# Where the first values are asked for: ScalarE's queue for two sets of values, and the third pair's q and k ahead of the second pair's values

## The chip, the core and the metric

The kernel runs on one core of a Trainium2 chip. The core has five engines that run their own instruction streams in order and wait for each other by semaphores: TensorE (PE, matrix products; PEld are its weight loads), VectorE (DVE), ScalarE (ACT), GpSimd (POOL) and SyncE (SP), which here only issues transfers. Transfers between HBM and the core's memory (SBUF) run on 16 DMA engines. The metric is the time of one execution on the device in microseconds (us); smaller is better.

## What is computed

Attention over 4 batches, 8 heads, 576 positions and 64 columns per head, a dense two-layer network with a softmax-weighted activation on its 2304 rows, and a mixture of eight experts. The shortened reference:

```
scores = (q @ k.T) / 8                      # per batch and head, 576 x 576
heads 0-3: keep 0 <= i - j < 32             # local heads
heads 4-7: keep i >= j and i % 32 == j % 32 # strided heads
attn = softmax(scores) @ v                  # -> x, 2304 x 512
h = x @ w_in                                # w_in 512 x 1024, float64
solu = h * softmax(h); ln = layernorm(solu) * g_ln
x = ln @ w_out                              # w_out 1024 x 512, float64
e = argmax(x @ w_gate + modality_bias[modality_id])
out = p_e * (relu(x @ w1[e]) @ w2[e])       # 8 experts
```

## The kernel before

Heads are worked on two at a time. A pair (batch, two heads) has a tile of q (`qn`), of k (`kn`) and of v (`vn`); 16 pairs are done in the order of `order` in `attention_slots` (L623). For batch 0 the order is two strided pairs first, then two local pairs. "The first pair" and "the second pair" below are the two strided ones, "the third" is the first local one. For each pair TensorE transposes q and k (into `ptq`; ScalarE copies them to `qT` and `kz`), forms scores (`S`), VectorE, ScalarE and GpSimd make the softmax (`exc` and `pc` for the first two pairs, `ex` and `pT` for the others), and TensorE multiplies by the values (into `po`, `bank`, `poy`); ScalarE and VectorE then split the result into a high and a low part (`xTH`, L496, and `xTL`, L497).

Beside that runs the preparation of w_in. It arrives as eight pieces of 128 x 1024 words (halves of float64 numbers, 512 KB each, tile `raw`). `f64_piece` makes float32 of a piece: a product `mag` on ScalarE (L292) or GpSimd (L294), two or three bit operations on VectorE (L301, L302, L304), then a cast on ScalarE (L312, `winH`) and a difference on VectorE or GpSimd (L314, `winL`). The pieces of w_out are prepared by the same function.

What sets the order: the kernel is written as a list of steps (`STAGES`, `W_IN_AT` and other tables of numbers), and a scheduler of the framework then orders each engine's instructions by a model of their durations. Buffers come from pools: `vn` has two, `qn` and `kn` together three (the second pair's k lies elsewhere), the `raw` tiles three and some borrowed ones. An instruction that needs a buffer waits until its last user is done. Each transfer also takes one of eight completion semaphores in turn (`DMAHW0` to `DMAHW7` in the rows of the order below) and waits, on the engine that issues it, for the transfer that had the same semaphore before, eight transfers earlier.

The start is set by the list `START` (L88): `q0` means `load_pair` of the first pair, which asks for q and k and, for the first two pairs, keeps the request for v back; `v0` issues that request (`get(v, vn)`, four transfers of 72 KB, L367); `r0` asks for the first piece of w_in. Behind it stand the four transpositions of the first pair. All these transfers are issued by SyncE. The third pair's `load_pair` comes later, out of `stage_t`, when the second pair's transposition is written. For a local pair, `load_pair` asks for q, k (L388) and v (L395, L397) together, GpSimd clears a corner of `vn` (L393), and `shift_values` copies parts of it within SBUF (L406).

Of the kernel before, what the change touches and what calls it, by code (L numbers as in the profile page):

```python
# [9 lines left out]
F32 = mybir.dt.float32  # L10
F32R = mybir.dt.float32r
I32 = mybir.dt.int32
U32 = mybir.dt.uint32
AF = mybir.ActivationFunctionType
ALU = mybir.AluOpType
# [13 lines left out]
def tile_attention_moe_moe2(  # L29
# [15 lines left out]
    nc = tc.nc  # L45
    B, H, S, D = q.shape
    NT, DM = out.shape
    NE, _, FF = w1.shape
    P = 128
# [8 lines left out]
    QUAD = 32  # L58
    RES = STRIDE // SG
    NR = SP_ // RES  # L60
# [20 lines left out]
    MAG_ON = 'AAAPAAPAAPPPAAPA'  # L81
    SIGN_ON = 'DDDDDDDDDDDDDDDP'
    W_IN_LOW = 'DDDDDPDP'
    LOW_ON = 'PPDDDPDD'
    KN1_HOME = True
    ANCHOR = False
    EXS = 4
    START = ['q0', 'q1', 'r0', 'r1', 'v0', 'v1']  # L88
    COMPACT_ON = 'P'
    E_BUFS = 2  # L90
    SO_BUFS = 2
# [74 lines left out]
    def warm(n, after=False):  # L166
        wide = ident.bitcast(mybir.dt.bfloat16)
        for _ in range(n):
            mm = nc.tensor.matmul(warm_out, wide[:, 0:P], wide, start=True, stop=True)
            if after and last_mm[0]:  # L170
                queue_after(mm, last_mm[0])
            last_mm[0] = mm
# [9 lines left out]
    def note(x):  # L182
        newest[x.ins.engine] = x

    def behind_newest(x):
        if ANCHOR and x.ins.engine in newest:
            queue_after(x, newest[x.ins.engine])

    def build_masks():
# [93 lines left out]
            nc.sync.dma_start(raw, w_out32[:, f])  # L283
            raw_out[f] = raw

    def f64_piece(raw, tm, tw, by_act, sgn="D"):
        hi, lo = raw[:, :, 1], raw[:, :, 0]
        mag = mp.tile([P, 512], F32, name="mag", tag=tm, bufs=TAG_BUFS.get(tm, 2))
        w = mp.tile([P, 512], F32, name="wf", tag=tw, bufs=TAG_BUFS.get(tw, 2))
        wi = w.bitcast(I32)  # L290
        if by_act:
            behind_newest(nc.scalar.activation(mag, hi.bitcast(F32), AF.Copy, scale=REBIAS))  # L292
        else:
            behind_newest(nc.gpsimd.tensor_tensor(  # L294
                mag, hi.bitcast(F32), rebias.to_broadcast([P, 512]), ALU.mult))
        if sgn == "P":
            nc.gpsimd.tensor_tensor(hi.bitcast(F32), hi.bitcast(F32), zeros.to_broadcast([P, 512]), ALU.mult)
            behind_newest(nc.vector.scalar_tensor_tensor(
                wi, mag.bitcast(I32), 3, hi, ALU.logical_shift_left, ALU.bitwise_or))
        else:  # L300
            behind_newest(nc.vector.tensor_scalar(wi, mag.bitcast(I32), 3, None, ALU.logical_shift_left))  # L301
            nc.vector.scalar_tensor_tensor(  # L302
                wi, hi, -2147483648, wi, ALU.bitwise_and, ALU.bitwise_or)
        nc.vector.scalar_tensor_tensor(  # L304
            wi, lo, 29, wi, ALU.logical_shift_right, ALU.bitwise_or)
        return w

    def prep_w_in(i):
        c, hf = divmod(IN_ORDER[i], 2)
        cs = slice(hf * 512, hf * 512 + 512)  # L310
        w = f64_piece(raw_in.pop(i), IN_MAG_TAG, "so", MAG_ON[i] == "A", SIGN_ON[i])
        nc.scalar.copy(winH[:, c, cs], w)  # L312
        low = nc.gpsimd if W_IN_LOW[i] == "P" else nc.vector
        low.tensor_tensor(winL[:, c, cs], w, winH[:, c, cs].bitcast(F32), ALU.subtract)  # L314
# [37 lines left out]
    def load_pair(b, hp, v_later=None):  # L352
# [8 lines left out]
        if hp >= H // 4:  # L361
            def get(src, dst):
                dst = dst[:, 0:2 * SG * D].rearrange("p (h x) -> p h x", h=2)
                if b == 0 and src is v:
                    parts = src[b, h0:h0 + 2].rearrange("h (a r i) d -> r a h (i d)", r=RES, i=SG)
                    for r in range(RES):
                        loaded[n_] = nc.sync.dma_start(dst[r * QUAD:r * QUAD + NR], parts[r])  # L367
                else:
                    loaded[n_] = nc.sync.dma_start(
                        dst[:SP_], src[b, h0:h0 + 2].rearrange("h (p i) d -> p h (i d)", i=SG))  # L370

            loaded[n_] = None
            get(q, qn)
            get(k, kn)
            if v_later:
                v_later.append(lambda: get(v, vn))
            else:
                get(v, vn)
            return qn, kn, vn[:, 0:2 * SG * D].rearrange("p (h t d) -> p h t d", h=2, d=D)
# [242 lines left out]
    def attention_slots():  # L622
# [6 lines left out]
        nat, tr, live = {}, {}, {}  # L629

        def load(n):
            if n < len(order):
                nat[n] = load_pair(*order[n])

        def transpose(n, part):
            if n < len(order):
                if part == 0:
                    tr[n] = alloc_pair(n, order)
                transpose_part(*order[n], part, *nat[n][0:2], *tr[n])
                if part == 3 and order[n][1] < H // 4:  # L640
                    shift_values(nat[n][2])

        late_v = [[None], [None]]
        for what in START:
            n_ = int(what[1])
            if what[0] == "q":
                nat[n_] = load_pair(*order[n_], late_v[n_])
            elif what[0] == "v":
                late_v[n_][1]()
            else:  # L650
                fetch_w_in(n_)
        for part in range(4):
            transpose(0, part)
            warm(WARM)
        pts = {}

        def stage_a(n):
# [929 lines left out]
```

## Time and profile before

| | us |
|---|---|
| median of 3 runs (lowest to highest) | 641.71 (638.81 to 642.04) |
| the profiled execution | 641.9 |
| its span | 640.2 |
| TensorE busy in the span | 597.3 |
| VectorE, ScalarE, GpSimd busy | 350.9, 278.6, 133.2 |

The span is the stretch of the profile from the first to the last recorded work; the profiled execution's own time is 1.7 us longer. Times in the rows below are counted from the span's start. The granted clock of TensorE (PEclk) is given as a share of its full 2.4 GHz; a DMA share is the mean busy share of the 16 DMA engines, which can be a little above one where packets overlap.

### The profile page before, as it was taken

The numbers are of one execution on the slowest core, as the hardware profiler recorded it, in microseconds if no ns is written. First come the engines' busy times: TensorE is split into PE (matmuls) and PEld (weight loads), VectorE is DVE, ScalarE is ACT, GpSimd is POOL, SyncE is SP. The second block draws the span as 40 slices with busy tenths as digits, with TensorE's granted clock in tenths as the row PEclk, the third lists the DMA queues.
The fourth block names the chain that finished last, engine by engine and source line by source line (L and its number), as shares of the span: only waits on it lengthen the run. The fifth ranks groups of instructions, "written<-read, shape, count | busy, mean of one in ns | idle before, by whom it ended". The sixth has DMA issues, their size and how long they took to land. (4 is left out here: it accounts for less than half of the span.)

```text
span 640.2 us, 14649 instructions
## 1 busy us (share of the span) xinstructions
PE 597.3 (93%) x5675; PEld 532.5 (83%) x5675; DVE 350.9 (55%) x1058; ACT 278.6 (44%) x653; POOL 133.2 (21%) x197
## 2 busy tenths in 40 slices
PE   6468899999999999999999999999999999999992
PEld 5356678998889988889888999989888888899892
DVE  6695696498567975677388744117264553121120
ACT  4345675555554656545165522124335352221220
POOL 2234221021011231024023412310111203012101
PEclk9999889999999999999999999999999999999997
DMA  7846540033322124110045200445456463012010
GB/s 203 249 136 170 152 121 21 20 90 95 105 55 55 38 72 110 38 36 17 18 136 160 84 34 23 117 159 158 148 165 198 132 203 101 21 51 67 22 44 24
DMA packets 48435, 61.65 MB, mean 96 GB/s; under 512 B 29361, under 2 KB 32971, under 8 KB 48333
## 3 DMA queue, kind: packets, MB, share of 16 engines
q1 hardware_dynamic: 41469, 44.09, 24.4%
q0 software_dynamic: 4272, 11.57, 5.7%
q10 hardware_dynamic: 2592, 4.72, 2.0%
q8 instruction: 53, 0.87, 0.6%
q14 instruction: 49, 0.40, 0.2%
HBM read 48.40 MB, written 10.26 MB: 92 GB/s over the span
## 5 line engine op out<-in xcount | busy, mean ns | idle before, releaser
L1146 PE MATMUL py<-w2H,winL 128*128 128x512 f32 x288 | 91.8, 395 | 0.0
L1190 PE MATMUL pf<-xTH,w1H 128*128 128x256 f32 x288 | 82.2, 286 | 1.0 <-DVE yo L1294 1.0
L1190 PE MATMUL pf<-xTL,w1H 128*128 128x256 f32 x288 | 81.7, 284 | 0.6 <-DVE xTL L1125 0.6
L1190 PE MATMUL pf<-xTH,w1L 128*128 128x256 f32 x288 | 81.5, 283 | 0.0
L1197 DVE SCALAR_TENSOR_TENSOR winL<-pf,winL 128x512 fp32r<-128x512 f32 x36 | 24.9, 692 | 95.2 <-ACT winL L1196 95.1
L1146 PEld LDWEIGHTS py<-w2H,winL 128*128 128x128 f32 x288 | 53.5, 188 | 10.6
L715 PE MATMUL ph<-winH,xTH 128*128 128x512 f32 x144 | 60.3, 419 | 1.2 <-DVE so L732 1.2
L1196 ACT ACTIVATE winL<-pf 128x512 fp32r<-128x512 f32 x36 | 21.5, 598 | 87.2 <-PE pf L1190 87.2
L715 PE MATMUL ph<-winL,xTH 128*128 128x512 f32 x144 | 58.3, 405 | 0.0
L1190 PEld LDWEIGHTS pf<-xTH,w1H 128*128 128x128 f32 x288 | 56.3, 196 | 2.2 <-ACT yo L1292 1.4
L1190 PEld LDWEIGHTS pf<-xTL,w1H 128*128 128x128 f32 x288 | 56.3, 196 | 1.3 <-DVE xTL L1125 1.0
L715 PE MATMUL ph<-winH,xTL 128*128 128x512 f32 x144 | 57.2, 402 | 0.0
L1190 PEld LDWEIGHTS pf<-xTH,w1L 128*128 128x128 f32 x288 | 56.3, 196 | 0.0
L1156 POOL DMA_INDIRECT out_dram<-yo,idx x14 | 14.1, 1004 | 141.3 <-ACT yo L1153 123.7
L797 PE MATMUL pa<-woH,nH 128*128 128x264 f32 x144 | 42.2, 293 | 1.0 <-ACT nH L786 1.0
L797 PE MATMUL pa<-woH,nL 128*128 128x264 f32 x144 | 42.6, 296 | 0.1
L797 PE MATMUL pa<-woL,nH 128*128 128x264 f32 x144 | 41.3, 287 | 0.0
L797 PE MATMUL pb<-woH,nH 128*128 128x256 f32 x144 | 41.1, 285 | 0.0
L797 PE MATMUL pb<-woH,nL 128*128 128x256 f32 x144 | 41.0, 285 | 0.0
L797 PE MATMUL pb<-woL,nH 128*128 128x256 f32 x144 | 40.7, 283 | 0.0
L559 POOL TENSOR_TENSOR ex<-ex,rd 72x288 f32<-72x288 f32 (+2 forms) x28 | 18.8, 673 | 76.6 <-DVE rd L550 45.9
L715 PEld LDWEIGHTS ph<-winH,xTH 128*128 128x128 f32 x144 | 27.9, 194 | 6.7 <-DVE so L732 1.7
(297 smaller groups left out, 1529.3 us busy)
## 6 DMA issues: line engine op xcount, KB each, us to landing
raw<-in_moe_w_dram SPq DMA_DIRECT2D x36, 512.0 KB
y_d<-yt ACTq DMA_DIRECT2D x18, 256.0 KB
raw<-in_moe_w_in_dram SPq DMA_DIRECT2D x8, 512.0 KB
raw<-in_moe_w_out_dram SPq DMA_DIRECT2D x8, 512.0 KB
qn<-in_q_dram SPq DMA_DIRECT2D x8, 288.0 KB
kn<-in_k_dram SPq DMA_DIRECT2D x8, 288.0 KB
qn<-in_q_dram SPq DMA_DIRECT2D x16, 144.0 KB
kn<-in_k_dram SPq DMA_DIRECT2D x16, 144.0 KB
```

Of the source, the lines that this page charges most:

```text
L559: note(nc.gpsimd.tensor_tensor(ex, ex, rd.unsqueeze(2).to_broadcast([nq, nt, nk]), ALU.mult))
L715: nc.tensor.matmul(ph, a[:, c, ts_], w[:, c, cs], start=n == 0, stop=n == 3 * KD - 1)
L797: nc.tensor.matmul(p, a[:, f], w[:, f, cols], start=n == 0, stop=n == 3 * KF - 1)
L1146: mm_ = nc.tensor.matmul(p, a[:, f, s], x, start=n == 0, stop=n == 3 * KF - 1)
L1156: nc.gpsimd.indirect_dma_start(out=out[:, :], out_offset=indirect(idx[:, col, 2:3].bitcast(U32)), in_=o, in_offset=None, bounds_check=NT - ...
L1190: mm = nc.tensor.matmul(p[:, u], a[:, c, fs], x[:, c], start=n == 0, stop=n == 3 * KD - 1)
L1196: last[0] = (nc.scalar.activation(hH[:, f2s], p, AF.Relu), nc.vector.scalar_tensor_tensor(hL[:, f2s], p, 0.0, hH[:, f2s].bitcast(F32), ALU ...
L1197: nc.vector.scalar_tensor_tensor(hL[:, f2s], p, 0.0, hH[:, f2s].bitcast(F32), ALU.max, ALU.subtract))
```

## The change

`START` is written anew, the first two pairs' values are issued by ScalarE (`V_QUEUE`), and `load` leaves out a pair that is loaded already. `t0` in the list stands for the four transpositions of the first pair, which stood behind the list. The parameter `ANCHOR` becomes a tuple of pieces; empty, it does nothing, as `False` did.

```
-    ANCHOR = False
+    ANCHOR = ()
+    V_QUEUE = 'scalar'
     EXS = 4
-    START = ['q0', 'q1', 'r0', 'r1', 'v0', 'v1']
+    START = ['q0', 'q1', 'r0', 'v0', 'r1', 't0', 'q2', 'v1']
...
                     for r in range(RES):
-                        loaded[n_] = nc.sync.dma_start(dst[r * QUAD:r * QUAD + NR], parts[r])
+                        loaded[n_] = getattr(nc, V_QUEUE).dma_start(dst[r * QUAD:r * QUAD + NR], parts[r])
...
         def load(n):
-            if n < len(order):
+            if n < len(order) and n not in nat:
                 nat[n] = load_pair(*order[n])
...
-            if what[0] == "q":
-                nat[n_] = load_pair(*order[n_], late_v[n_])
+            if what[0] == "t":
+                for part in range(4):
+                    transpose(0, part)
+                    warm(WARM)
+            elif what[0] == "q":
+                nat[n_] = load_pair(*order[n_], late_v[n_] if n_ < 2 else None)
             elif what[0] == "v":
                 late_v[n_][1]()
             else:
                 fetch_w_in(n_)
-        for part in range(4):
-            transpose(0, part)
-            warm(WARM)
```

`q2` asks for all three tensors of the third pair. Line numbers after the change are one or two higher. The values of the third pair take the second buffer of `vn`, so those of the second pair take the first pair's buffer.

SyncE at the start of the program, before (72 rows are a strided pair's q and k, 96 a local pair's, 18 the first two pairs' values, 128x1024 a piece of w_in):

```order
L369 DMA qn<-in_q_dram 72x2x512
L369 DMA kn<-in_k_dram 72x2x512
L369 DMA qn<-in_q_dram 72x2x512
L369 DMA kn<-in_k_dram 72x2x512
L277 DMA raw<-in_moe_w_in_dram 128x1024 x2
L367 DMA vn<-in_v_dram 18x2x512 x8
L277 DMA raw<-in_moe_w_in_dram 128x1024
L388 DMA qn<-in_q_dram 96x2x192 x2
L388 DMA kn<-in_k_dram 96x2x192 x2
L388 DMA qn<-in_q_dram 96x2x192 x2
```

The same place after the change, with the semaphores that each row waits for (a third transfer of values, of 64 rows, then the third and another piece follow):

```order
L370 DMA kn<-in_k_dram 72x2x512
L370 DMA qn<-in_q_dram 72x2x512
L370 DMA kn<-in_k_dram 72x2x512
L278 DMA raw<-in_moe_w_in_dram 128x1024 [waits DMAHW0_49]
L278 DMA raw<-in_moe_w_in_dram 128x1024 [waits DMAHW1_49]
L389 DMA qn<-in_q_dram 96x2x192 [waits DMAHW2_49,PE_49]
L389 DMA qn<-in_q_dram 96x2x192 [waits DMAHW3_49]
L389 DMA kn<-in_k_dram 96x2x192 [waits DMAHW4_49,PE_49]
L389 DMA kn<-in_k_dram 96x2x192 [waits DMAHW5_49]
L396 DMA vn<-in_v_dram 128x4x64 [waits DMAHW6_49]
L396 DMA vn<-in_v_dram 128x4x64 [waits DMAHW7_49]
```

The eight transfers of values have left SyncE, and the third pair's q, k and values stand ahead of the third piece of w_in; the first two pieces now wait for one landing each, since ScalarE's four transfers have taken four of the eight semaphores.

ScalarE some 38 us into the run, at the end of the first pair's products with values, before:

```order
L292 ACTIVATE mag<-raw 128x512
L312 CAST winH<-wf 128x512
L496 CAST xTH<-po 128x18x4
L496 CAST xTH<-bank 128x18x4
L496 CAST xTH<-poy 128x18x4 x2
L446 COPY kz_112<-ptq 64x288 x2
```

And after:

```order
L497 CAST xTH<-po 128x18x4
L293 ACTIVATE mag<-raw 128x512
L497 CAST xTH<-bank 128x18x4
L497 CAST xTH<-poy 128x18x4
L313 CAST winH<-wf 128x512
L368 DMA vn<-in_v_dram 18x2x512 x4
L497 CAST xTH<-poy 128x18x4
L447 COPY kz_112<-ptq 64x288 x4
```

The second pair's values are issued there; the first pair's are ScalarE's first instructions.

GpSimd some 43 us into the run, up to the softmax of the third pair (`ex`; `mag` are products for pieces of w_out, `tabi` a table that is cleared), before:

```order
L234 MEMSET tabi 128x176x2
L235 MEMSET tabi 128x176
L314 TENSOR_TENSOR winL<-wf,winH 128x512
L474 TENSOR_TENSOR exc<-exc,rd 128x4x18
L533 TENSOR_TENSOR ex<-ex,mx 128x256
L294 TENSOR_TENSOR mag<-raw,rebias 128x512 x2
L559 TENSOR_TENSOR ex<-ex,rd 128x256
```

And after:

```order
L235 MEMSET tabi 128x176x2
L236 MEMSET tabi 128x176
L315 TENSOR_TENSOR winL<-wf,winH 128x512
L475 TENSOR_TENSOR exc<-exc,rd 128x4x18
L295 TENSOR_TENSOR mag<-raw,rebias 128x512 x2
L534 TENSOR_TENSOR ex<-ex,mx 128x256
L560 TENSOR_TENSOR ex<-ex,rd 128x256
```

The two products of w_out have moved from behind the first subtraction to ahead of it.

## Rows read from the trace of the kernel before

**Rows 1.** Page, span in 40 slices: busy tenths of TensorE, its clock

```profile
PE   6468899999999999999999999999999999999992
PEclk9999889999999999999999999999999999999997
```

**Rows 2.** Stretches (us): length, busy us of engines (count), PEclk, DMA share, GB/s

```profile
0.00:66.00 66.00, 41.12 (x909) 33.44 (x911) 44.27 (x143) 29.14 (x83) 21.39 (x59) 1.00 0.68 191
66.00:70.00 4.00, 4.00 (x71) 2.86 (x63) 1.28 (x6) 3.63 (x10) 1.26 (x3) 0.57 0.71 175
...
90.80:97.60 6.80, 6.54 (x49) 5.15 (x48) 5.72 (x20) 5.67 (x16) 1.98 (x3) 0.52 0.16 46
97.60:640.00 542.40, 526.54 (x4470) 474.68 (x4468) 281.56 (x839) 225.34 (x504) 103.46 (x125) 0.99 0.28 83
```

**Rows 3.** Stretches of the start, the same columns (PE, PEld, DVE, ACT, POOL)

```profile
11.20:13.70 2.50, 1.96 (x40) 1.65 (x40) 2.50 (x10) 1.91 (x6) 0.32 (x1) 1.00 0.74 164
...
16.00:20.30 4.30, 0.00 (x0) 0.00 (x0) 0.26 (x2) 0.01 (x1) 0.00 (x0) 1.00 1.08 240
20.30:25.30 5.00, 4.68 (x134) 4.09 (x134) 4.31 (x20) 3.92 (x10) 1.36 (x3) 1.00 1.01 334
```

**Rows 4.** Timeline of SyncE: start, us, line, tile<-source, count

```profile
3.56 8.37 SPq L367 DMA_DIRECT2D vn<-in_v_dram  x8
...
12.82 0.81 SPq L388 DMA_DIRECT2D qn<-in_q_dram  x2
...
21.12 0.34 SPq L277 DMA_DIRECT2D raw<-in_moe_w_in_dram  x1
...
50.00 0.33 SPq L283 DMA_DIRECT2D raw<-in_moe_w_out_dram  x1
...
61.16 2.10 SPq L391 DMA_DIRECT2D qn<-in_q_dram  x2
```

**Rows 5.** Waits of SyncE until 60 us: us in total, times, longest

```profile
SPq L367 <- DMA kn<-in_k_dram: 2.3, 2, 1.2
SPq L367 <- DMA raw<-in_moe_w_in_dram: 2.0, 2, 1.1
```

**Rows 6.** Timeline near 20 us, three engines; in brackets idle time before and its releaser

```profile
20.29 0.66 ACT L292 ACTIVATE mag<-raw 128x512 f32<-128x512 f32 x1 [5.35 <-DMA raw<-in_moe_w_in_dram]
...
20.61 1.57 PE L158 MATMUL ptq<-ident,qn 96*64 96x96 f32 x12 [5.26 <-DMA qn<-in_q_dram]
...
20.99 0.43 DVE L301 TENSOR_SCALAR wf<-mag 128x512 int32<-128x512 int32 x1 [4.73 <-ACT mag L292]
```

**Rows 7.** Timeline near 27 us, GpSimd and VectorE

```profile
26.92 1.04 POOL L294 TENSOR_TENSOR mag<-raw,rebias 128x512 f32<-128x512 f32 x1 [1.53 <-DVE rd L469]
...
28.00 0.96 DVE L301 TENSOR_SCALAR wf<-mag 128x512 int32<-128x512 int32 x2 [1.14 <-POOL mag L294]
```

**Rows 8.** Stretch from 30 to 40 us, columns of rows 2

```profile
30.00:40.00 10.00, 5.17 (x116) 4.42 (x116) 9.55 (x24) 6.44 (x20) 2.47 (x4) 1.00 0.34 108
```

**Rows 9.** Timeline: ScalarE, TensorE and VectorE around the second pair's products with values

```profile
39.23 0.36 ACT L496 CAST xTH<-poy 128x72 fp32r<-128x72 f32 x2
...
42.17 0.39 PE L158 MATMUL po<-pc,vn 18*64 18x18 f32 x2 [4.03 <-DVE xTL L497]
...
49.07 0.19 DVE L497 TENSOR_TENSOR xTL<-po,xTH 128x72 fp32r<-128x72 f32 x1
```

**Rows 10.** Timeline around the third pair's first softmax

```profile
50.55 0.61 POOL L533 TENSOR_TENSOR ex<-ex,mx 128x256 f32<-128x256 f32 x1 [1.74 <-DVE mx L529]
...
52.97 0.18 DVE L550 RECIPROCAL rd<-den 128x4 f32<-128x4 f32 x1
...
53.09 1.04 POOL L294 TENSOR_TENSOR mag<-raw,rebias 128x512 f32<-128x512 f32 x1 [0.18 <-DMA raw<-in_moe_w_out_dram]
...
54.75 0.69 PE L154 MATMUL pP<-ident,ex 128*128 128x128 f32 x2
```

**Rows 11.** Timeline of TensorE at 65 us

```profile
65.38 0.44 PE L154 MATMUL ptq<-ident,qn 96*128 96x96 f32 x3 [2.55 <-DMA qn<-in_q_dram]
```

More of the change, by code (lines that the diff above doesn't have):

```diff
@@ L183, in note, with behind_newest @@
         newest[x.ins.engine] = x
-    def behind_newest(x):
-        if ANCHOR and x.ins.engine in newest:
+    def behind_newest(x, piece):
+        if piece in ANCHOR and x.ins.engine in newest:
             queue_after(x, newest[x.ins.engine])
@@ L284, in fetch_w_out, with f64_piece @@
             raw_out[f] = raw
-    def f64_piece(raw, tm, tw, by_act, sgn="D"):
+    def f64_piece(raw, tm, tw, by_act, sgn="D", piece=None):
         hi, lo = raw[:, :, 1], raw[:, :, 0]
@@ L291, in f64_piece @@
         if by_act:
-            behind_newest(nc.scalar.activation(mag, hi.bitcast(F32), AF.Copy, scale=REBIAS))
+            behind_newest(nc.scalar.activation(mag, hi.bitcast(F32), AF.Copy, scale=REBIAS), piece)
         else:
             behind_newest(nc.gpsimd.tensor_tensor(
-                mag, hi.bitcast(F32), rebias.to_broadcast([P, 512]), ALU.mult))
+                mag, hi.bitcast(F32), rebias.to_broadcast([P, 512]), ALU.mult), piece)
         if sgn == "P":
@@ L298, in f64_piece @@
             behind_newest(nc.vector.scalar_tensor_tensor(
-                wi, mag.bitcast(I32), 3, hi, ALU.logical_shift_left, ALU.bitwise_or))
+                wi, mag.bitcast(I32), 3, hi, ALU.logical_shift_left, ALU.bitwise_or), piece)
         else:
-            behind_newest(nc.vector.tensor_scalar(wi, mag.bitcast(I32), 3, None, ALU.logical_shift_left))
+            behind_newest(nc.vector.tensor_scalar(wi, mag.bitcast(I32), 3, None, ALU.logical_shift_left), piece)
             nc.vector.scalar_tensor_tensor(
@@ L310, in prep_w_in @@
         cs = slice(hf * 512, hf * 512 + 512)
-        w = f64_piece(raw_in.pop(i), IN_MAG_TAG, "so", MAG_ON[i] == "A", SIGN_ON[i])
+        w = f64_piece(raw_in.pop(i), IN_MAG_TAG, "so", MAG_ON[i] == "A", SIGN_ON[i], i)
         nc.scalar.copy(winH[:, c, cs], w)
```

## The prediction

> **What bounds the kernel now.** I read three views in this order: the forty slices of the page, stretches of the span side by side, and the timeline of single engines over the first 66 us. The slices show TensorE near full from the fourth slice on and two dips of its clock [rows 1]. The stretches show the same in numbers: TensorE is busy 41.12 of the first 66 us, and 526.54 of the 542.40 us from 97.6 on [rows 2]. So the end of the run is set by how early TensorE becomes continuously busy; a microsecond won before 66 us is carried to the end, unless a later wait or the clock takes it. The change reorders only the start (and, through the scheduler, small things after it), so the start is where it must pay.
>
> In the start three things wait together at 20 us. TensorE waits 5.26 us for the third pair's q, ScalarE waits 5.35 us for the third piece of w_in, and VectorE waits 4.73 us for the product that ScalarE makes of that piece [rows 6]. The reason is the transfers. SyncE needs from 3.56 us on 8.37 us to issue the eight transfers of values [rows 4], because from the third of them on each waits for an earlier transfer to land (the waits name k, w_in and q) [rows 5]; the third pair's q goes out at 12.82 us, and the DMA engines are then full: share 1.08 at 240 GB/s from 16.0 to 20.3 us [rows 3]. After that VectorE sets the pace. It is busy 9.55 of the 10 us from 30 to 40 [rows 8], and TensorE waits for what it writes, 4.03 us at 42.17 for instance [rows 9]. VectorE's stream has one more gap on the way, 1.14 us before 28.00, for a product of GpSimd that began at 26.92, when the fourth piece of w_in had landed [rows 7] (the row names a reciprocal of VectorE, but in the program this product waits for nothing but its piece).
>
> **The change part by part.** *Values of the first pair on ScalarE's queue, the third pair's q and k moved up.* The transfers that SyncE issues before the third pair's q fall from fifteen (four q and k, two pieces, eight values, one piece) to six. The first two pieces now each wait for an earlier transfer to land. With sizes from the shapes (288 KB for each of a pair's q, k and v, 512 KB a piece) 2752 KB are then ahead of and in it (four q and k 1152, first values 288, two pieces 1024, q 288), where it was 3552 KB. At 240 GB/s [rows 3] the 800 KB less are 3.4 us, so q lands near 17 us, and TensorE's 5.26 us shrink to about 2. If TensorE set the pace here, that would be the gain.
>
> *But VectorE's and ScalarE's wait is for the third piece, and that one moves behind more.* Before, by 20.6 us 3840 KB had landed: four q and k (1152), two pieces (1024), both values (576), the third piece (512), and the third pair's q and k (576). After, the third piece has in front of it q and k of three pairs (1728), the first values (288), two pieces (1024) and the third pair's values (288): with its own 512 that is 3840 KB again. What can be won is the stretch from 11.2 to 13.7 us, where the eight small transfers of values moved only 164 GB/s [rows 3]: against 240 that is 2.5 x (1 - 164/240) = 0.8 us. So the third piece lands at about 19.5, and ScalarE, with the exponentials of the softmax queued behind its product in program order, still stands there. In that wait VectorE has by the new order done seven more of its small operations (like the one of 0.19 us [rows 9]), 1.3 us.
>
> *The fourth piece takes most of that back.* All of VectorE's work behind the wait at 28.00 is the same list before and after in another sequence; only an earlier fourth piece starts it earlier. Up to that piece 5664 KB were moved before; after, the second pair's values (288) are gone, the third pair's values (288) have come, and two of the third pair's shifts inside SBUF (144 KB) are asked for ahead of it: 5808 KB. 144 KB at the 334 GB/s of that stretch [rows 3] are 0.4 us, against the 0.8 won: the piece is 0.4 us earlier. It is asked for only when the third piece has landed, before at 21.12 [rows 4], now near 20. Bounds: 0.2 us later (the third pair's values, in rows of 256 bytes, move at the 164 GB/s of the small transfers, which costs 0.6 on their 288 KB), 2.1 us earlier (all that VectorE saves before it, 0.8 + 1.3, if the piece is in time for it). I take -0.4, the sum of the bytes; the rest of the 2.1 turns into a longer wait at the same place.
>
> *The second pair's values.* They take the buffer of the first pair's, so they are issued by ScalarE when the first pair's products with values are done. In the rows of before ScalarE finishes the copies of that step at 39.23 + 0.36 [rows 9]; with the new order's -0.4 it is 39.2. Nothing shows a landing of such a transfer alone; the fourth piece took 5.8 us from its issue at 21.12 [rows 4] to 26.92 [rows 7], full engines and all. So the values are there between 39.2 and 45.0, where TensorE began these products at 42.17 [rows 9]: 0 to 2.8 us late. VectorE needs their result only at 49.07 [rows 9], so I take that as hidden, nothing; without that cover up to 2.8 would be paid. ScalarE's eight issues cost some 0.4 each (two of SyncE's took 0.81 [rows 4]) and lie before its first copy and behind a copy whose successors wait for TensorE: nothing; at most 1.6 us each time.
>
> *GpSimd's order.* Two products of w_out pieces now stand ahead of the first subtraction of the local softmax, where they stood behind it. Before, that subtraction began at 50.55, the second product at 53.09, and TensorE transposed the normalised result at 54.75 without a gap [rows 10]. From the subtraction's end at 51.16 VectorE's reciprocal was ready at 53.15 [rows 10], 2.0 later, and the normalising product takes another 0.61: 3.2 us from the subtraction's start to the transposes. After, the subtraction waits until the later of the two pieces has landed and been multiplied. If that ends at 52 (the pieces are asked for up to 2 us earlier), the transposes come at 55.2, 0.5 later; if at 54.13 as before, at 57.3, 2.6 later. Bounds 0 and 2.6 us; I take 1, nearer to the earlier. The cover is TensorE's own wait of 2.55 us at 65.38 for the q of the sixth pair [rows 11], which hangs on SyncE's queue (issue at 61.16 [rows 4]) and not on this. So 1 costs nothing, and of 2.6 some 0.1 would show, or 0.7 if SyncE's 0.6 below comes too.
>
> *SyncE's queue behind it.* A w_out piece went out at 50.00 after waiting for the table's store; after, another buffer frees it, and everything behind it to the q of 61.16 can move up, by 0 to 2 us. I take 0.6, since the second pair's last products still gate the values between.
>
> Sum: -0.4 at VectorE, 0 for the values, 0 for GpSimd, -0.6 at SyncE: -1.0. The profiled execution is 641.9 us, its span 640.2, and the median of the runs 641.71. 641.9 - 1.0 = 640.9; taken to the median, 640.7.
>
> **Two rules beside this.** Beside the row of 16.0 to 20.3 us, where one queue alone had the DMA engines at share 1.08, stands the Trainium skill, "DMA: Bandwidth & Descriptors", section "Issuing engines are not separate DMA queues": transfers from ScalarE and SyncE run on the same sixteen engines, so a second queue saves issue time only. The trace agrees there; by the rule alone the move is worth nothing, and the sum would be the 0.6 of SyncE's queue. The Trainium skill, the same page, section "Why a DMA increments its semaphore by 16 and not by 1", says that a transfer uses the largest number of engines up to 16 that divides its rows: nine for the 18 rows of these values. The 164 GB/s beside 240 fit that. By it (an estimate) the nine engines carry a third more while the first q and k (twelve engines for 72 rows) are loaded beside the first values, 96 + 32 KB each in place of 96, and the first piece's product comes later by up to 2 us, which the wait at 20 us hides.
>
> **The rivals.** *Returned in full:* the third piece lands with the q, near 17 us, because transfers share the engines instead of following each other; the wait at 20.99 loses 3.5 us and the fourth piece 3. For it: third piece and q landed within 0.3 us of each other before [rows 6]. Against it: the sum of bytes. 641.9 - 3.0 - 1.2 = 637.7. *The clock:* TensorE ran at half clock from 66 to 70 (mean 0.57) and 90.8 to 97.6 (0.52) [rows 2], the first behind the wait at 65.38, the lower of its levels being 1.2 of 2.4 GHz. Such a stretch costs 4.00 x 0.43 = 1.7 or 6.54 x 0.48 = 3.1 us. If the changed waits spare one, 640.9 - 2.4 = 638.5. *Slower:* GpSimd stands in front of the first local softmax for the second w_out piece until 54.13 or later, and TensorE idles over 3 us at its transposes; from 2.55 us on the cover is used up. With 1 us beyond it, and a third stretch at half clock behind that idle time (3.1, as the longer of the two), it is 641.9 - 0.4 + 1.0 + 3.1 = 645.6. For it: the row at 65.38 shows such an idle time ahead of such a stretch. Against it: the 5.26 us at 20 us have none behind them [rows 1]. *Not what it says:* the third pair's q still waits for landings of earlier transfers, so that it is not ahead by time at all; the start is as before, 641.9.
>
> **How the numbers follow.** Forecast (-1.0, own range 639 to 642.5) 0.47; returned in full 0.16; one stretch of low clock spared 0.13; slower 0.14; as before 0.10. Within 0.5%, about what a measurement of this kernel can tell from no change, is 638.5 to 644.9. Faster than that: most of the returned case (0.13) and half of the clock (0.07) with 0.05 from the forecast's edge, 0.25. Slower: two thirds of that rival, 0.09, and 0.02 for unknown ones, 0.11. Same 0.64. The range 636.5 to 645 leaves about 0.1 on either side.
>
> **What would show it.** Right: TensorE's wait near 15 to 20 us is below 3 us; ScalarE's wait for the third piece still ends at 19 to 20; the wait before 28 us grows to about 3 and ends within 1 us of 28.0; the second pair's products begin near 42 without a stall that VectorE repeats; GpSimd's first local subtraction comes after two products, 1 to 2 us later; the wait at 65 ends 1 us earlier. Wrong: the fourth piece's product begins before 25.5, or the wait at 65 is gone while TensorE's transposes near 55 come after 57.

## The result, and the profile after

| | before | after |
|---|---|---|
| median, us | 641.07 (637.81 to 642.21, 19 runs) | 644.19 (641.82 to 648.46, 19 runs) |
| ratio to before | 1 | 1.0062, 95% interval 1.0045 to 1.0080 |
| profiled execution / its span | 641.9 / 640.2 | 648.5 / 646.7 |

The change made the kernel slower by 0.6%, where 640.7 us was forecast and no clear change was held the likeliest (0.64). The profiled execution of after is the slowest of its 19 runs, 4.3 us above their median; so a second profile of the same kernel, from a later run, is used beside it (its execution was 644.0 us, close to that median).

The slices of after, TensorE and its clock, against [rows 1]:

```profile
PE   5559999999999999999999999999889999999992
PEclk9999999999999999999999999999999999999997
```

Dips of TensorE's busy share have come in the 29th and 30th slice (from 453 us on). The clock looks better than before, but its products say otherwise for 59 to 70 us: three 96x96 transposes took 0.74 us at 59.21, 61.29 and 67.14, and 0.48 again at 71.02, where the same form took 0.44 at 65.38 before [rows 11]. The reason is that the trace has no record of the clock ahead of 71.1 us in after, and of 56.3 us in before, and that its rows read 1.00 there. By the products TensorE ran at half clock until then: pairs of transposes (96x96, 64 columns) follow each other 0.15 us apart from 19 to 55 us in after and from 21 to 53 us in before, and 0.075 us apart in a later profile (after, with eight instructions taken off ScalarE) whose record does read 1.00 there:

```profile
52.69 0.72 PE L159 MATMUL ptq<-ident,kn 96*64 96x96 f32 x12
```

Twelve of them took 1.23 us at 18.69 in after (row below) and 1.57 at 20.61 in before [rows 6]. So the clock rose 14.8 us later in after than in before.

Stretches of after, columns as in [rows 2, 3]:

```profile
0.00:66.00 66.00, 42.42 (x854) 33.85 (x856) 42.24 (x138) 27.70 (x77) 20.96 (x57) 1.00 0.69 190
66.00:70.00 4.00, 4.00 (x53) 3.31 (x48) 1.40 (x5) 2.02 (x6) 0.85 (x2) 1.00 0.33 75
97.60:640.00 542.40, 528.20 (x4476) 475.77 (x4474) 284.32 (x848) 228.76 (x513) 105.52 (x128) 1.00 0.28 83
...
11.20:13.70 2.50, 2.13 (x70) 1.70 (x68) 0.12 (x1) 0.15 (x1) 0.00 (x0) 1.00 0.93 268
16.00:20.30 4.30, 3.81 (x105) 3.07 (x109) 4.11 (x16) 3.78 (x9) 0.63 (x1) 1.00 0.85 270
20.30:25.30 5.00, 3.73 (x123) 3.02 (x118) 4.94 (x21) 2.75 (x8) 2.23 (x4) 1.00 0.93 254
```

TensorE is busy longer in the first 66 us and yet has done less: 854 products against 909; and of 66 to 70 us, 53 against 71, although the clock of that row reads 1.00 (without a record) and before's 0.57. Of the first stretches, 11.2 to 13.7 moves 268 GB/s where it moved 164, as hoped; but 20.3 to 25.3, in which the fourth piece travels, moves 254 where it moved 334, at a DMA share that is hardly smaller (0.93 and 1.01).

SyncE's issues and its waits until 66 us, against [rows 4, 5]:

```profile
4.52 1.69 SPq L278 DMA_DIRECT2D raw<-in_moe_w_in_dram  x2
8.22 0.82 SPq L389 DMA_DIRECT2D qn<-in_q_dram  x2
...
15.89 1.59 SPq L278 DMA_DIRECT2D raw<-in_moe_w_in_dram  x2
...
20.92 0.53 SPq L278 DMA_DIRECT2D raw<-in_moe_w_in_dram  x1
```

```profile
SPq L278 <- DMA raw<-in_moe_w_in_dram: 2.5, 2, 1.5
SPq L389 <- DMA kn<-in_k_dram: 1.9, 1, 1.9
SPq L278 <- DMA vn<-in_v_dram: 1.9, 1, 1.9
```

The first two pieces are asked for at 4.52 instead of 2.66, behind the landing of earlier transfers. The third pair's q is asked for at 8.22 instead of 12.82, and the fourth piece at 20.92 instead of 21.12. So the request for the fourth piece is on time, but the piece isn't. The timeline near 20 and near 30 us, against [rows 6, 7]:

```profile
18.69 1.23 PE L159 MATMUL ptq<-ident,qn 96*64 96x96 f32 x12
20.73 0.68 ACT L293 ACTIVATE mag<-raw 128x512 f32<-128x512 f32 x1 [0.45 <-DMA raw<-in_moe_w_in_dram]
21.57 0.38 DVE L302 TENSOR_SCALAR wf<-mag 128x512 int32<-128x512 int32 x1
```

```profile
29.73 1.04 POOL L295 TENSOR_TENSOR mag<-raw,rebias 128x512 f32<-128x512 f32 x1 [4.77 <-DMA raw<-in_moe_w_in_dram]
```

```profile
30.80 0.85 DVE L302 TENSOR_SCALAR wf<-mag 128x512 int32<-128x512 int32 x2 [4.94 <-POOL mag L295]
```

The three waits of about 5 us at 20 us are gone. A part of them has moved ahead: ScalarE's product of the first piece began at 13.55 behind a wait of 2.87, where it began at 10.24 before behind one of 1.55. And a new one stands at the fourth piece: VectorE's wait has grown from 1.14 to 4.94 us and ends at 30.80 instead of 28.00, 2.80 us late. From there VectorE is busy again (9.13 of 30 to 40 us [rows 8], 9.56 of 40 to 50), and nothing gives this back by 57 us. The second pair's products with values and the first local softmax, against [rows 9, 10]:

```profile
40.81 0.66 ACTq L368 DMA_DIRECT2D vn<-in_v_dram  x2
43.33 0.79 PE L159 MATMUL po<-pc,vn 18*64 18x18 f32 x11 [4.77 <-DMA vn<-in_v_dram]
51.41 1.04 POOL L295 TENSOR_TENSOR mag<-raw,rebias 128x512 f32<-128x512 f32 x1
52.64 1.04 POOL L295 TENSOR_TENSOR mag<-raw,rebias 128x512 f32<-128x512 f32 x1 [0.19 <-DMA raw<-in_moe_w_out_dram]
53.64 0.61 POOL L534 TENSOR_TENSOR ex<-ex,mx 128x256 f32<-128x256 f32 x1
55.40 0.18 DVE L551 RECIPROCAL rd<-den 128x4 f32<-128x4 f32 x1
57.03 0.66 PE L155 MATMUL pP<-ident,ex 128*128 128x128 f32 x2
```

TensorE transposes at 57.03 instead of 54.75: 2.28 us late. To see where the rest of the 6.5 us comes from, two marks serve: the column sums of w_out (`csum`, 119.60 us before) and ScalarE's last output of the first expert group (`yo<-py,idxE`, 429.19 before), behind which the experts' stage runs to the end. Of before and, in the second fence, of after:

```profile
119.60 0.38 ACT L824 COPY csum<-pa 128x264 f32<-128x264 f32 x1 [0.88 <-PE pa L821]
429.19 0.69 ACT L1153 ACTIVATE yo<-py,idxE 128x512 f32<-128x512 f32 x1 [3.12 <-PE py L1146]
```

```profile
121.25 0.38 ACT L826 COPY csum<-pa 128x264 f32<-128x264 f32 x1 [0.27 <-PE pa L823]
430.97 0.69 ACT L1155 ACTIVATE yo<-py,idxE 128x512 f32<-128x512 f32 x1 [3.12 <-PE py L1148]
```

So 1.65 us at 121, 1.78 at 431, and 6.5 at the end: 4.7 of the 6.5 us arise behind 431 us, where the change moves no instruction. TensorE's waits from 428 us on, before:

```profile
PE pf L1190 <- DVE yo L1294: 1.0, 1, 1.0
PE pq L1233 <- ACTq L1550: 0.9, 1, 0.9
PE pf L1190 <- DVE xTL L1125: 0.6, 2, 0.3
```

and after:

```profile
PE pf L1192 <- ACT winH L1053: 3.0, 1, 3.0
PE pq L1235 <- ACTq L1552: 1.6, 1, 1.6
PE pf L1192 <- DVE yo L1291: 1.5, 1, 1.5
PE pf L1192 <- ACT yo L1290: 1.3, 1, 1.3
```

`ACTq` is ScalarE's sequencer: at L1550 (L1552) the program takes a branch, and TensorE's first product behind it waits for ScalarE's side. The experiments follow this wait up as a second cost. In this profile it is a small part: the rows add up to 4.9 us more than before's, and the branch has 0.7 of them. The other three waits of after stand at 471.7, 506.5 and 541.5 us; in its second profile TensorE waits 0.5 us or less at each of these places and 2.10 at the branch. So they did not come back with the kernel, and the wait at the branch did.

### The profile page after: what moved, and what is told of

It is laid out like the page before. It is cut to its first block, busy times and chain, and to the rows that moved or that the text cites. A ratio compares the mean times of both kernels' runs of the same rounds, so it can differ in the third digit from the quotient of the medians.

```text
span 646.7 us, 14644 instructions
## 1 busy us (share of the span) xinstructions
PE 600.3 (93%) x5675; PEld 534.5 (83%) x5675; DVE 350.4 (54%) x1058; ACT 279.6 (43%) x653; POOL 134.0 (21%) x197
```

## The experiments

Each ratio is to runs of before on the same chip, with its 95% interval. "Pieces" are pieces of w_in. `RAW_HOME` names for each piece the set of buffers it uses.

**Which part of the change costs? Four kernels.** The values on ScalarE's queue alone, before's order kept:

```
-    START = ['q0', 'q1', 'r0', 'v0', 'r1', 't0', 'q2', 'v1']
+    START = ['q0', 'q1', 'r0', 'r1', 'v0', 'v1', 't0']
```

> The values of both first pairs on ScalarE's queue from the start, the third pair's tensors left where they were before. Theory S (supply: the third pair's values and their shifts stand ahead of the fourth piece of w_in, so that piece lands 2.8 us later, and VectorE, which sets the pace to 60 us, carries it): nothing of that is left here, so the fourth piece's product on GpSimd begins at 27 or earlier, and the time is 0.997 to 1.002 of before. Theory F (first loads: ScalarE's values share the engines with the first q and k, which land 1 to 2 us later, and VectorE's start is what costs): k of the first pair lands as late as after the change or later (8.3 us or more), and the time is 1.002 to 1.006 of before.

655.72, ratio 1.0229 (1.0190 to 1.0268). ScalarE issued the eight transfers until 11.03 us, loaded its table behind them and made its first copy at 12.35 (6.66 in after). It also loses some 5 us between 97 and 120 us, of which below.

Everything but the queue:

```
-    V_QUEUE = 'scalar'
+    V_QUEUE = 'sync'
```

> The changed kernel with the values issued by SyncE; the list of the start is the changed one. Theory S: the third pair's values and shifts are still ahead of the fourth piece, its product begins at 28.5 or later, and the time is 1.003 to 1.008 of before. Theory F: the first q and k land as before the change (k transposes at 6.3), and the time is 0.998 to 1.002 of before.

642.81, ratio 1.0028 (1.0003 to 1.0052). The fourth piece's product on GpSimd, and VectorE behind it:

```profile
27.79 1.04 POOL L295 TENSOR_TENSOR mag<-raw,rebias 128x512 f32<-128x512 f32 x1 [2.26 <-DMA raw<-in_moe_w_in_dram]
...
28.87 0.43 DVE L302 TENSOR_SCALAR wf<-mag 128x512 int32<-128x512 int32 x1 [2.28 <-POOL mag L295]
```

28.87 lies 0.87 behind before and 1.93 ahead of after. By this pair of profiles the list's order costs the first, ScalarE's queue the second (one execution each; of streams equal up to 57 us, this wait ended at 30.80, 30.90 and 30.03 in the three profiles with after's and at 28.00 and 27.50 in the two with before's). The wait at the branch is 0.87, as before.

The third pair left where it was, and the second pair's values ahead of it:

```
-    START = ['q0', 'q1', 'r0', 'v0', 'r1', 't0', 'q2', 'v1']
+    START = ['q0', 'q1', 'r0', 'v0', 'r1', 't0', 'v1']
```

> The changed kernel without the third pair in the list of the start: its q, k and values come from where they came before. Theory S: the fourth piece's product begins at 27.5 or earlier, and the time is 0.997 to 1.002 of before. Theory F: the first q and k are as late as after the change (k at 8.3), and the time is 1.002 to 1.006. Theory B (the second pair's values wait for the first pair's buffer, and TensorE's 4.8 us of waiting for them is what costs): that wait is gone, and with it the loss, 0.997 to 1.002.

```
+    START = ['q0', 'q1', 'r0', 'v0', 'r1', 't0', 'v1', 'q2']
```

> The changed kernel with the second pair's values asked for ahead of the third pair: they have their own buffer again, and it is the third pair's values that wait for the first pair's; its q and k stay early. Theory S: its values and shifts are behind the fourth piece, whose product begins at 27 or earlier, and the time is 0.994 to 1.001 of before. Theory F: 1.002 to 1.006, with the first k at 8.3. Theory B: as S; the two are told apart by the stretch of 20 to 31 us, where by B nothing but the third pair's own wait changes and VectorE's wait for GpSimd's product ends near 30.8.

652.84, ratio 1.0174 (1.0133 to 1.0216), and 652.16, ratio 1.0176 (1.0141 to 1.0210). Both bring the fourth piece earlier than after does (27.31 and 27.49) and lose some 5 us between 97 and 120 us, as the first kernel did: the scheduler had put two exponentials ahead of the gate's copies on ScalarE, and TensorE waited there, in the first of the two:

```profile
106.85 1.13 PE L345 MATMUL pg<-wg,wt 128*128 128x8 f32 x8 [1.82 <-ACT wt L342]
```

with a stretch at half clock behind it (107.7 to 114.5). So none of the three isolates a part of the change. To test that reading, the last of them was run with the exponentials held behind the newest gate copy:

```
+            if gated:
+                queue_after(x, gated[max(gated)])
```

> The kernel in which the second pair's values stand ahead of the third pair lost 5 us between 97 and 120 us, where ScalarE does two exponentials of the dense layer ahead of the gate's columns, so that TensorE stands at the gate's products and runs at half clock behind that. Here those exponentials are held behind the gate's columns, as before the change. Theory O (a difference of order that the scheduler makes there, and not the start, costs those 5 us): 1.004 to 1.012 of before, and TensorE's waits for the copies of the gate near 107 are gone. If it is the start: 1.014 or more.

657.58, ratio 1.0265 (1.0233 to 1.0298): this held the exponentials of the dense network too, 9 to 30 us late from 77 us on. It tells nothing of the cause at 97 us, which stays a reading of the trace.

**The change once more, and the fourth piece asked for first.**

> The changed kernel once more, for a second profile of it on the chip of the three runs beside it. All theories: 1.004 to 1.008 of before; VectorE's wait for the fourth piece ends at 30.8 within 0.2 us again (transfers and order repeat), while the stretches of low clock between 56 and 110 us and the waits of the experts' stage from 450 to 550 us may lie otherwise; if the 4.9 us that the first profile lost in that stage belong to the kernel and not to the execution, they are there again.

645.69, ratio 1.0077 (1.0050 to 1.0105). In this execution VectorE's wait was 5.18 and ended at 30.90, and the transposes came at 57.47; the 96x96 transposes took 0.74 us at 59.77 and 61.84 and 0.47 from 66.82 on (the record of the clock begins at 65.6), one stretch at half clock of 3.4 us (93.0 to 96.4) followed, where before had 3.4 and 6.8, and the column sums came at 119.39, 0.21 ahead of before. The start's loss repeats; what is left of it at 120 us differs by 1.9 us between two executions of one kernel, and their stretches at half clock differ too.

```
-    RAW_HOME = 'rrnnrnrn'
+    RAW_HOME = 'rrnrnnrn'
```

The same in after, and in before:

> The changed kernel with the buffers of the fourth and the fifth piece of w_in exchanged, so that the fourth piece is asked for right behind the third and the fifth waits in its place. Theory S (VectorE's wait for the fourth piece is what the change costs): its product begins at 25 or earlier, VectorE's wait ends 4 us or more before 30.8, the first local softmax comes 1.5 us or more earlier than after the change, and the time is 0.995 to 1.002 of before. If the piece is only one of many late things: the wait moves to the fifth or sixth piece, and the time stays at 1.003 to 1.008.

> The kernel before with the same exchange of buffers. Theory S: VectorE's wait of 1.14 us before 28 goes, little else can be won, 0.996 to 1.001 of before. If VectorE does not set the pace there: 0.999 to 1.004.

641.45, ratio 1.0021 (0.9994 to 1.0048), and 642.16, ratio 1.0019 (0.9999 to 1.0040). In after with this edit:

```profile
22.95 1.46 POOL L295 TENSOR_TENSOR mag<-raw,rebias 128x512 f32<-128x512 f32 x1 [1.89 <-DMA raw<-in_moe_w_in_dram]
...
24.45 0.52 DVE L302 TENSOR_SCALAR wf<-mag 128x512 int32<-128x512 int32 x1 [0.67 <-POOL mag L295]
...
54.55 0.69 PE L155 MATMUL pP<-ident,ex 128*128 128x128 f32 x2
```

The wait of 4.94 is 0.67, and the transposes come at 54.55, 0.20 ahead of before. GpSimd's two products of w_out still stand ahead of its subtraction in this kernel, and the second pair's values still go out on ScalarE (37.75): neither of them costs anything up to these transposes. In before, the same edit makes GpSimd stand 3.57 us for a piece of w_out (52.17) and wins nothing. In after with this edit the wait behind the branch was 2.12, and the experts' stage was 2.2 us longer than before.

The values on SyncE, and the fourth piece first:

```
-    V_QUEUE = 'scalar'
+    V_QUEUE = 'sync'
-    RAW_HOME = 'rrnnrnrn'
+    RAW_HOME = 'rrnrnnrn'
```

> The changed list of the start with both changes that the runs so far point to: the values issued by SyncE and the fourth piece of w_in asked for right behind the third. Theory S with C (C: with the values on ScalarE's queue, ScalarE's code behind the branch near 452 us comes 0.1 to 1.2 us later than the 0.6 us after that branch that every kernel with the values on SyncE showed, and a stretch at half clock can follow): TensorE's idle time at that branch is 0.87 again, the first softmax of the third pair is not later than before, and the time is 0.994 to 1.000 of before. If C is chance from run to run: idle time there of 1.0 or more, and 0.998 to 1.004.

639.17, ratio 0.9990 (0.9966 to 1.0014): level with before, and the best of all. Holding GpSimd's w_out products behind the first normalising product, in before and in this kernel, each with the fourth piece first:

```
...
+            if first_norm and tm == "nH":
+                queue_after(x, first_norm[0])
...
```

> The kernel before with the fourth piece asked for behind the third, as in the run that came out level with before, and GpSimd's products of w_out held behind the first softmax of the third pair. In that earlier run GpSimd stood 3.6 us for a piece of w_out with the first subtraction behind it, and VectorE was 1.9 us late at 53 us. Theory G (that standing gave back what the earlier fourth piece had won): the first subtraction begins at 50.5 or earlier, VectorE is early by 1 us or more at 53, and the time is 0.994 to 1.000 of before. If the gain is lost elsewhere: 0.999 to 1.004.

> The same two edits on the changed list of the start with the values on SyncE. If the third pair's early q, k and values are worth anything once nothing else is late: faster than the same edits on the kernel before, 0.992 to 0.998 of before; by theory S alone, which sees no gain for TensorE while VectorE sets the pace: level with it, 0.996 to 1.001.

641.20, ratio 1.0011 (0.9991 to 1.0032), and 641.67, ratio 1.0012 (0.9989 to 1.0035). The first subtraction came at 46.92 and 46.21 instead of 50.55, and VectorE was 4 to 5 us ahead at 53 us; at the transposes that stand at 56.89 us in before TensorE was 0.9 and 0.1 behind it, so nothing of it lasts. No version beats before.

**Eight more instructions on ScalarE.** The change gives ScalarE eight more to issue. In before, eight copies of one column each do so, with one clearing on GpSimd ahead of them:

```
+    pad = cst.tile([P, 9], F32, name="pad")
+    nc.gpsimd.memset(pad[:, 0:1], 0.0)
+    for i in range(8):
+        nc.scalar.copy(pad[:, i + 1:i + 2], pad[:, 0:1])
```

> The kernel before with eight copies of one column added at ScalarE's start, where it has nothing to do until 5.5 us. Theory C by the place of the code (ScalarE's instructions behind the branch are shifted by the eight issues, and must be loaded when it gets there): TensorE's idle time at the branch near 452 us grows from 0.87 to 1.0 us or more, and the time is 1.001 to 1.005 of before. If it is ScalarE's queue of transfers and not the place of the code: 0.87 again, and 0.998 to 1.002.

645.04, ratio 1.0065 (1.0039 to 1.0091), as much as the whole change; the wait behind the branch was 1.45. Then eight other issues of ScalarE (the first eight outputs of the dense network) were given to SyncE, in after, in after with the fourth piece first, in before with the eight copies, and in before:

```
-        nc.scalar.dma_start(y_d[1 + t * P:1 + (t + 1) * P, :], yt)
+        (nc.sync if t < 8 else nc.scalar).dma_start(y_d[1 + t * P:1 + (t + 1) * P, :], yt)
```

> The changed kernel with the issues of the first eight tiles of y moved from ScalarE to SyncE (124 to 230 us), so that ScalarE has as many instructions ahead of the branch near 452 us as before the change; the start is the same. Theory C (place of ScalarE's code): TensorE's idle time at the branch is 0.87 to 0.92 again, what is lost between 440 and 640 us falls from 2 to 5 us to under 1, and the time is 1.000 to 1.004 of before, what is left being the start. Theory S alone: 1.005 to 1.009.

> The same on the changed kernel with the fourth piece asked for behind the third. By S and C together nothing of the loss is left: 0.995 to 1.000 of before. If the issues on SyncE cost something of their own, or C is wrong: 1.001 to 1.005.

> The kernel before with the eight copies on ScalarE that cost 0.65%, and eight issues of y taken off it. By C the count is what it was: idle time of 0.87 at the branch, 0.998 to 1.002 of before. If the copies cost by what they do at the start: 1.004 to 1.009 again.

> The kernel before with only the eight issues of y moved to SyncE: ScalarE's code is shorter by eight. By C its place is another one again, with an idle time at the branch that may be 0.87 or longer; if the issues on SyncE are free and the code there does not matter: 0.998 to 1.002 of before.

641.65, ratio 1.0016 (0.9991 to 1.0041); 643.18, ratio 1.0038 (1.0009 to 1.0067); 644.19, ratio 1.0063 (1.0036 to 1.0089); 641.24, ratio 1.0022 (1.0002 to 1.0042). The branch's wait was 0.87 in all four. In after this took off most of the loss although the start stayed 2.3 us late at 57. In before with the copies it took off nothing of the time, so the copies cost by something besides the branch. In after with the fourth piece first it took off nothing either (1.0021 without it, 1.0038 with it, where 0.995 to 1.000 had been expected).

The last of the four shows how far single marks can be trusted. Up to 57 us ScalarE, VectorE, GpSimd and SyncE have the same instructions in the same order there as in before, and yet TensorE's transposes came 1.72 us later (54.75 before), because GpSimd waited longer for pieces of w_out (0.72 and 0.18 in before):

```profile
53.05 1.04 POOL L294 TENSOR_TENSOR mag<-raw,rebias 128x512 f32<-128x512 f32 x1 [2.21 <-DMA raw<-in_moe_w_out_dram]
54.81 1.04 POOL L294 TENSOR_TENSOR mag<-raw,rebias 128x512 f32<-128x512 f32 x1 [0.72 <-DMA raw<-in_moe_w_out_dram]
...
56.47 0.69 PE L154 MATMUL pP<-ident,ex 128*128 128x128 f32 x2 [1.99 <-POOL ex L559]
```

Two more kernels were to put the copies in the middle of the run, in before and in the level kernel (values on SyncE, fourth piece first):

```
+        if t == 8:
+            for i in range(8):
+                nc.scalar.copy(pad[:, i:i + 1], rebias)
```

> The kernel before with eight one-column copies on ScalarE, issued behind the ninth tile's output (about 235 us), ahead of the branch near 452 us; the start is untouched. Theory C (eight more instructions on ScalarE cost through where the code behind them falls, seen at the branch): the offset at 57 and 124 us within 0.5 us of before, the wait of PE behind the branch 1.0 or more where before has 0.87, experts' stage 212 to 216 us long (before 211.0), time 1.003 to 1.008 of before. Theory S (the copies of the earlier run cost by what they do at the start): wait 0.87, stage 211, time 0.999 to 1.002.

> The kernel with the values on SyncE's queue and the fourth piece asked for first (0.999 of before, its PE wait behind the branch 0.91), with the same eight copies behind the ninth tile's output. Theory C: wait behind the branch 1.0 or more, experts' stage 212 to 216 us (210.5 without the copies), time 1.003 to 1.006 of before. Theory S: 0.997 to 1.001 and a stage of 211.

646.84, ratio 1.0094 (1.0062 to 1.0125), and 649.11, ratio 1.0141 (1.0113 to 1.0170). They did not run midway. The instructions of tile `pad` in the second:

```profile
L816 ACT COPY pad<-rebias x8: 186/187/191, 2.2 to 2.8; 128x1 f32<-128x1 f32 x8
```

Start times of 2.2 to 2.8 us: nothing orders the copies behind anything, and the scheduler took them to the front. So place and start are not told apart; what the two give is the price again, in another kernel too. In the second of them TensorE's first product behind the branch, against the same kernel without the copies (second fence):

```profile
455.04 0.58 PE L1239 MATMUL pq<-winH,xTH 128*128 128x256 f32 x1 [3.73 <-ACTq L1556]
```

```profile
450.10 0.36 PE L1235 MATMUL pq<-winH,xTH 128*128 128x256 f32 x1 [0.91 <-ACTq L1552]
```

and the stretches from 452 us on, the first of which holds most of that wait, with the copies and, in the second fence, of before:

```profile
452.00:456.00 4.00, 0.96 (x4) 0.96 (x5) 0.00 (x0) 0.40 (x1) 0.29 (x1) 0.71 0.41 155
456.00:460.00 4.00, 4.00 (x21) 4.00 (x20) 0.00 (x0) 0.39 (x1) 0.69 (x1) 0.50 0.16 66
```

```profile
452.00:456.00 4.00, 3.13 (x27) 3.12 (x27) 0.00 (x0) 1.07 (x2) 0.00 (x0) 1.00 0.58 205
456.00:460.00 4.00, 4.00 (x33) 3.92 (x33) 0.85 (x2) 1.75 (x5) 0.98 (x1) 1.00 0.17 68
```

The wait is 2.8 us longer, and from 453.6 to 460.5 TensorE has half clock: with both, 25 products in 8 us against 60. That one place costs this kernel 5.3 us: its lag on the level kernel grows from 2.1 to 7.4 us within 6 us.

Where each pays, as differences of the marks named above, one execution each (before is the base of all but the last, whose base is the level kernel):

| kernel | transposes (54.75) | column sums (119.60) | output (429.19) | stage behind it (211.0) | wait at branch |
|---|---|---|---|---|---|
| after | +2.28 | +1.65 | +1.78 | +4.7 | 1.61 |
| after again | +2.72 | -0.21 | -0.15 | +2.2 | 2.10 |
| after, fourth piece first | -0.20 | +0.19 | +0.46 | +2.2 | 2.12 |
| after, eight fewer | +2.33 | +0.74 | +0.65 | -0.1 | 0.87 |
| before, eight fewer | +1.72 | +1.15 | +1.49 | +0.1 | 0.87 |
| before, eight copies | +0.39 | +0.08 | +0.52 | +3.0 | 1.45 |
| before, eight copies (second form) | +1.09 | +3.66 | +4.12 | +4.1 | 2.04 |
| level kernel, eight copies | +1.29 | +1.38 | +1.92 | +7.0 | 3.73 |

Where ScalarE has eight instructions more, the experts' stage is 2.2 to 7.0 us longer here; where eight others are taken off, it is not. (In the four kernels with the values on ScalarE and another list it was 0.8, 1.2, 0.7 and 5.6 longer, with waits of 1.0, 1.8, 1.0 and 4.4.) Two executions of one kernel, after and after again, are 2.5 us apart in this column. It does not go by the count alone; but where ScalarE's stream is no longer than before's, the stage was at most 0.3 longer, save 1.4 with the copies in and eight issues off.

## Why the prediction was wrong

**The step that failed** is the fourth piece, "I take -0.4, the sum of the bytes", with bounds of 0.2 us later and 2.1 earlier. It measured 2.80 later, outside them (28.00 to 30.80 at VectorE, 26.92 to 29.73 at the product). The time of the whole kernel lies in the range of 636.5 to 645, but on the other side of before. The sum of the bytes counted what lies in front of the piece and moved it at before's 334 GB/s from the old time on. Two things were left out. The first two pieces are themselves 1.9 us late in being asked for, since SyncE waits 1.9 for the first pair's values to land (the row L278 <- DMA vn above); the prediction noted that wait and gave it no price. And beside the fourth piece now travel the third pair's copies within SBUF, which went out from 42.73 us on before: two just ahead of it (19.41), which the sum has, and two behind it (22.97), which it hasn't; the stretch moved 254 GB/s, not 334. Whichever of the three profiles with after's streams is set against whichever of the two with before's, the wait ends 2.0 to 3.4 us later. The run with the values on SyncE puts 1.93 us of the 2.80 down to ScalarE's queue and 0.87 to the order of the list; how much of either is the late request of the first pieces and how much the company is not shown. The estimate by nine engines had the first piece's product up to 2 us later; it came 3.31 later (13.55 for 10.24), of which the later request is 1.86. The landing of a transfer was estimated where only its request was known: it was asked for 0.2 us earlier and was there 2.8 us later.

**A term that was missing.** The sum priced eight issues on ScalarE by their 0.4 us each and found cover for that; it had nothing for a branch 400 us later. Eight idle copies cost 0.65% and 0.94% in before, in two forms, and 1.5% in the level kernel (1.0141 for 0.9990); eight issues taken off brought after from 1.0062 to 1.0016. How much of after's loss belongs to each cause stays open: taking the late piece out leaves 1.0021, taking eight issues off leaves 1.0016, doing both leaves 1.0038, with intervals that overlap. That the branch is one place where ScalarE's extra instructions are paid is shown by the rows; that it is the only one is not: with the copies in and eight issues off, the branch was as before and the time still 1.0063, and in the first profile of after the branch has 0.7 of the 4.7 us that its last stage is longer.

**What held, and what else did not.** The wait for the third pair's q is gone. The third piece came later than the 19.5 expected: it was multiplied at 20.73, and ScalarE, which "still stands there", stood 0.45 us. The second pair's values made TensorE wait 4.77 us at 43.33, and that was hidden, as reckoned. GpSimd's subtraction did come behind two products, 3.09 us later, of which its order costs nothing: with the fourth piece early the transposes came 0.20 ahead of before. The wait at 65 us is gone, but as TensorE arrives later, not as SyncE is earlier (the q of 61.16 went out at 61.05): the -0.6 of that term was not there. That the wait goes while the transposes come after 57 (57.03) is a sign that the prediction had named for being wrong.

**The rivals.** The slower one had the right sign, size (645.6 against a median of 644.19) and a part of its shape, a longer wait with a stretch at half clock behind it; its place, GpSimd's w_out products, was wrong. Against a further stretch at half clock it was held that the wait of 5.26 us at 20 us has none behind it [rows 1]; that reading fails, since the trace has no record of the clock there and the products show half clock up to 53 us. The stretches of half clock before 120 us do move from one execution to the next, and in the second profile of after nothing is left of the start's loss at 119 us.

## What to carry to other kernels

A transfer that is asked for no later can land later: when requests are moved, follow each piece that paces an engine to the row of its first use, and price what travels beside it. Instructions that do nothing for the data path still cost where a later branch waits for their engine; count what a change adds to each engine's stream, above all ahead of a branch. Take a mark from more than one execution before a microsecond is built on it: equal streams put the same transposes 1.7 us apart here. And undo a part, or add a probe, only with a look at where the scheduler put it: of the runs here, three parts put back and three probes tested something else than they were meant to.

## What the runs showed of the hardware that was not expected

- The wait behind the branch is 0.87 to 0.91 us in each kernel whose ScalarE stream is no longer than before's, and 1.0 to 4.4 in the others. It is ScalarE that stands: from its branch to its next instruction 0.52 us in the first, 0.65 in the two with 1.0, and 1.11 to 3.77 in the rest. A page of the Trainium skill bears on it: "Runtime: NRT & Kernel Launch", section "Instruction fetch mechanics", says that a taken branch to code that isn't held yet makes the engine fetch it by DMA before it goes on. The traces agree with that: in the five profiles with 2.04 us or more, one to three transfers of 8 KB of the queue that the profile calls `instruction` began and ended while ScalarE stood, and in the others none did, save one with 1.82 us whose transfer ended with the wait. For which engine such a transfer is they don't say.
- Stretches at half clock began in this wait or within 1.5 us behind it in all five profiles in which it was 2.04 us or more (2.04, 2.10, 2.12, 3.73, 4.4), and in none of the others (1.82 at most).
- From 20 us on TensorE ran at half clock in every profile until its first recorded clock, which is full and begins at 50.9 to 75.5 us: ahead of it the 64-column transposes come 0.15 us apart, at full clock 0.075. It began at 56.3 us in before and at 65.2 in before with eight issues off ScalarE, whose streams are equal up to 57 us but for two of TensorE's products.
- The granted clock of a row isn't proof that the clock was up: where the trace has no record the row reads 1.00, in after up to 71.1 us, where equal products take 0.74 us in place of 0.41 to 0.48.
